# Two stores of the gradient of wo, split by partitions into two and three parts

## The chip, the core and the metric

The kernel is written in Bass with the Tile layer and runs on one core of one Trainium2 chip. Its time is the device time of one execution in microseconds; of the kernel before there are three such times, and one further execution was taken with the hardware profiler. A core has the engines PE (matmul), DVE, ACT and POOL, SP (which here only issues transfers), and 16 DMA engines, which move everything between the chip's memory (HBM) and the on-chip memory with its 128 partitions. SP and ACT each have a hardware queue for transfers (q1 and q10 in the profile), POOL has a software queue (q0); all three are served by the same 16 DMA engines.

## The reference

One transformer block for one decoded token, in bfloat16, forward and backward:

```
h  = x + attention(layernorm(x), k_cache, v_cache, wq, wo)      # 32 heads of 128, 4096 cached positions, batch 2
h2 = h + relu(layernorm(h) @ w1) @ w2                           # 640 -> 1728 -> 640
outputs: h2, and the gradients (for grad_out) of x, k_cache, v_cache, wq, wo, w1, w2
```

The caches are 67 MB each, and so are their gradients; the weights and their gradients are a few MB each. The gradient of wo is a matrix of 4096 x 640: for each batch the outer product of the attention output `o` (4096 long) with the gradient that reaches `h` (640 long), summed over the two batches.

## The kernel before, in words

Phase 1 runs over the 64 pairs of batch and head: it loads K and V of a pair (1 MB each), makes the scores, the softmax and the sums that the output needs. Phase 2 runs over the 64 pairs again in another order (`turns`): it takes V (`Wt`, loaded again except for twelve pairs that were kept), makes the gradient of the probabilities, and writes the gradients of V and K of the pair, `gV` and `gK`, 1 MB each, with `outer_half` on DVE (L843). These 128 stores are issued by POOL (L911 and L862) on the software queue, one after the other; a buffer of `gV` or `gK` is used again when its store has landed on all DMA engines.

Beside phase 2 run generators that a step counter advances by fixed rates (`bg_step`): `fin_gen` makes the gradients of the weights. It widens a column vector into rows (`rows_of`) and calls `outer_rows`, which fills an output tile `ot` by small matmuls (L972) and copies on ACT (L978), and stores it with a transfer that ACT issues (L981). `ot` has 128 partitions; for the gradient of wo (`out_5`) each partition holds 16 consecutive rows of one half of the matrix, and they go out in three groups that begin at c0 = 0, 6 and 12: 6, 6 and 4 rows of 640 numbers, that is 7680, 7680 and 5120 bytes per partition in one piece. The loop over `s0` does this for the two halves (L1009 to L1011). The order of all instructions is fixed when the program is built.

Loads are issued by SP (L463, L379, L1025), and so are the four short stores of the two small outputs (`store_row`, L664), each of 5 rows of 256 bytes. Every transfer of SP and ACT takes one of eight semaphores in turn, and waits until the transfer eight before it has landed. Each DMA engine that takes part in a transfer writes a small packet of 4 bytes to the semaphore when its share is done.

The lines that the text speaks of: L220 and L221 (two loads of 10 rows of 256 bytes at the start), L463 (`Kt`, `Vt`, `Wt`), L664, L843, L862, L911, L978, L981, L1009 to L1011.

Of the kernel before, what the change touches and what calls it, by code (L numbers as in the profile page):

```python
# [15 lines left out]
def kernel(  # L16
# [20 lines left out]
    nc = tc.nc  # L37

    B, Sq, D = A_x.shape
# [34 lines left out]
    def pst(shape, dtype, role, name):  # L74

        k = banks[role].pop(0)
        banks[role].append(k)
        return ps.tile(shape, dtype, tag=f"bank{k}", bufs=1, name=name)
# [11 lines left out]
    def take(tag, shape, name):  # L90
        assert free[tag] > 0, (tag, name)
        free[tag] -= 1
        k = homes[tag].pop(0)
        t = pools[k].tile(shape, BF16, tag=f"big{k}", bufs=1, name=name)
        home_of[id(t)] = (tag, k, t)
        return t
# [9 lines left out]
    def give(t, to=None, first=False):  # L106
        tag, k, _ = home_of.pop(id(t))
        to = to or goes_to(tag)
        owned[tag] -= 1
        owned[to] += 1  # L110
        free[to] += 1
        homes[to].insert(0 if first else len(homes[to]), k)
        given_at[k] = step[0]
# [8 lines left out]
    def rested(tag, n):  # L122

        return free[tag] > 0 and (forced[0] or step[0] >= given_at.get(homes[tag][0], -n) + n)
# [24 lines left out]
    def wait(n):  # L149

        end = step[0] + n * spread[0]
        while step[0] < end and not forced[0]:
            yield 0.0
        yield
# [763 lines left out]
    def rows_of(pool, col, n, name, tag):  # L918

        r = pool.tile([128, n * 128], BF16, tag=tag, bufs=2 if tag == "rD" else 1, name=name)  # L920

        def widen(c0):
            cn = min(4, n - c0)
            w = FIN["wide"][(c0 // 4) % 2]
            nc.scalar.copy(out=w[:, 0:cn, :, 0:B], in_=col[:, c0:c0 + cn, None, :].to_broadcast([128, cn, 4, B]))

        widen(0)
        yield
        yield
        for c0 in range(0, n, 4):  # L930
            cn = min(4, n - c0)
            w = FIN["wide"][(c0 // 4) % 2]
            o_busy.append(banks["o"][0])
            t = pst([128, 512], FP32, "o", "rw_ps")
            for k in range(cn):
                nc.tensor.matmul(t[:, k * 128:(k + 1) * 128], lhsT=w[:, k, :, :].rearrange("p q x -> p (q x)"),  # L936
                                 rhs=ident_bf[:], start=True, stop=True)
            nc.scalar.copy(out=r[:, c0 * 128:(c0 + cn) * 128], in_=t[:, 0:cn * 128])
            o_busy.pop(0)
            if c0 + 4 < n:  # L940
                widen(c0 + 4)
                yield 1.0
            yield 0.7
        FIN[name] = r

    FIN = {}
# [2 lines left out]
    spreading = [False]  # L949
    o_busy = []  # L950

    def outer_rows(L, r0, nrow, R, N, out_ap, cc):


        P = nrow // cc
        grp = max(1, min(cc, 4096 // N))
        out_v = out_ap.rearrange("(p c) n -> p c n", c=cc)
        for c0 in range(0, cc, grp):
            gn = min(grp, cc - c0)
            while not rested("f", 13):  # L960
                yield 0.0
            ot = take("f", [128, grp, N], "ot")
            todo = [(k, n0, min(512, N - n0)) for k in range(gn) for n0 in range(0, N, 512)]
            made = []
            for x in range(len(todo) + 1):
                if x < len(todo):
                    k, n0, nn = todo[x]
                    q = 32 * (fw[0] % 4)
                    o_busy.append(banks["o"][0])
                    o_ps = pst([128, 512], FP32, "o", "o_ps")  # L970
                    fw[0] += 1
                    nc.tensor.matmul(o_ps[0:P, 0:nn], lhsT=L[q:q + B, bass.ds(r0 + c0 + k, P, step=cc)],  # L972
                                     rhs=R[q:q + B, n0:n0 + nn], start=True, stop=True)
                    made.append((o_ps, k, n0, nn))
                    yield 0.3
                if x > 0:
                    o_ps, k, n0, nn = made[x - 1]
                    nc.scalar.copy(out=ot[0:P, k, n0:n0 + nn], in_=o_ps[0:P, 0:nn])  # L978
                    o_busy.pop(0)
                    yield 0.3  # L980
            nc.scalar.dma_start(out=out_v[:, c0:c0 + gn, :], in_=ot[0:P, 0:gn, :])  # L981
            give(ot)

    def fin_gen(fin):
        FIN["wide"] = [fin.tile([128, 4, 4, 32], BF16, tag="wide", bufs=2, name="wide") for _ in range(2)]
        for w in FIN["wide"]:
            nc.vector.memset(w[:], 0.0)
        yield from wait(2)
        yield from rows_of(fin, acol, NF, "ar", "rX")
        ar_ps = pst([128, NFF, B], FP32, "mid", "ar_ps")  # L990
        for cf in range(NFF):
            nc.tensor.matmul(ar_ps[:, cf, :], lhsT=FIN["ar"][0:B, bass.ds(cf, 128, step=NFF)], rhs=ident_bf[0:B, 0:B],
                             start=True, stop=True)
        nc.scalar.copy(out=arow[:, 0:NFF, :], in_=ar_ps[:])
        if F_rem:
            nc.scalar.copy(out=arow[:, NFF, :], in_=acol[:, NFF, :])
        yield ("arow", 0)
        yield from rows_of(fin, gc, ND, "gr", "rD")
        yield from outer_rows(FIN["ar"], 0, NFF * 128, FIN["gr"], D, out_7[0:NFF * 128, :], NFF)
        if F_rem:  # L1000
            yield from outer_rows(FIN["ar"], NFF * 128, F_rem, FIN["gr"], D, out_7[NFF * 128:Dff, :], 1)
        yield from rows_of(fin, ghfc, NF, "ghfr", "rX")
        yield from rows_of(fin, x2c, ND, "x2r", "rD")
        yield from outer_rows(FIN["x2r"], 0, D, FIN["ghfr"], Dff, out_6, ND)
        HH = H // 2
        while ("gh1", B - 1) not in done:
            yield
        yield from rows_of(fin, gh1c, ND, "gh1r", "rD")
        for s0 in range(0, H, HH):  # L1009
            yield from rows_of(fin, OFc[:, s0:s0 + HH, :], HH, "OFr", "rX")  # L1010
            yield from outer_rows(FIN["OFr"], 0, HH * 128, FIN["gh1r"], D, out_5[s0 * 128:(s0 + HH) * 128, :], HH)  # L1011
        yield from rows_of(fin, x1c, ND, "x1r", "rD")
        for s0 in range(0, H, HH):
            while not all(("go", B - 1, h) in done for h in range(s0, s0 + HH)):
                yield
            yield from rows_of(fin, GQc[:, s0:s0 + HH, :], HH, "GQr", "rX")
            yield from outer_rows(FIN["x1r"], 0, D, FIN["GQr"], HH * 128, out_4[:, s0 * 128:(s0 + HH) * 128], ND)
# [165 lines left out]
    for n, (i, j) in enumerate(plan):  # L1183
# [29 lines left out]
        if i is None and ("w1", 1) in done and fin is None:  # L1213
            wts.release()
            fin = tc.alloc_tile_pool(name="fin", bufs=1)
            big2 = tc.alloc_tile_pool(name="big2", bufs=1)
            more_home("f", big2)
            banks.update(sps=[2, 3], o=[4, 5, 6])
            bg2.append(("fin", fin_gen(fin)))
            bg3.append(("gx", gx_gen(fin)))  # L1220
# [23 lines left out]
        at = LIGHT if j is None else HEAVY_TAIL if open_tail else HEAVY  # L1244
# [63 lines left out]
```

## Time and profile before

| | |
|---|---|
| three runs | 891.62, 892.14 (median), 892.43 us |
| the profiled execution | 892.4 us, of which the span from the first to the last instruction is 890.6 us |
| busy in the span | PE 83%, DVE 77%, ACT 53%, POOL 23% |
| DMA | 361.84 MB in 56304 packets, 404 GB/s over the span |
| stores of `ot` | 19, issued by ACT from 568.2 to 843.2 us |

The profile has the busy time of every engine in 40 slices of the span, the share of the DMA engines that was busy and what they moved, the chain of waits that ended last, groups of instructions, and the transfers with their time from issue to landing. Times in the text are from the start of the span. The DMA share is a mean over the 16 DMA engines, so one engine alone shows as 0.06. Beneath the profile's views the trace has a record of every DMA packet: start, duration, queue and bytes. It does not name the DMA engine.

### The profile page before, as it was taken

Reading aid. Unit: us, or ns where it says so; the run is one execution under the profiler, and the core shown is the slowest. Engines: PE = TensorE matmul, PEld = TensorE weight load, DVE = VectorE, ACT = ScalarE, POOL = GpSimd, SP = SyncE. Lnnn points to the kernel's source line nnn. Section 1 sums busy time; section 2 is a strip of 40 time slices with the busy share of each in tenths; the row PEclk is TensorE's granted clock in tenths of the full one; section 3 lists DMA queues with packets and bytes.
Section 4 is the critical chain, followed back from the end, with each engine's and each line's share of the span. In section 5 each row is a group of like instructions: output and inputs, shape, how many; then the busy total and the mean of one; then the engine's idle time right before and its main releaser. Section 6 shows DMA issues by size and latency. Waiting matters only on the chain. (4 is left out here: it accounts for less than half of the span.)

```text
span 890.6 us, 24645 instructions
## 1 busy us (share of the span) xinstructions
PE 740.5 (83%) x10145; PEld 622.4 (70%) x10145; DVE 687.8 (77%) x1283; ACT 469.7 (53%) x1184; POOL 204.3 (23%) x342
## 2 busy tenths in 40 slices
PE   4999899999999998888888767885888888658871
PEld 4887788888887887777777656764666665536561
DVE  2665779876789897796796888786988467899992
ACT  1344334443455665454547766554567766437751
POOL 1344434342310000000023321121323011111141
PEclk9999989999999999997995555555557765555555
DMA  9999999999889999999999999999999999999995
GB/s 377 419 411 404 409 407 419 410 415 408 350 325 369 422 422 424 422 421 424 422 390 423 420 419 420 419 416 416 391 404 413 424 425 425 424 426 424 423 421 245
DMA packets 56304, 361.84 MB, mean 406 GB/s; under 512 B 5696, under 2 KB 11904, under 8 KB 15488
## 3 DMA queue, kind: packets, MB, share of 16 engines
q1 hardware_dynamic: 34536, 211.13, 58.1%
q0 software_dynamic: 18432, 134.23, 36.2%
q10 hardware_dynamic: 3224, 14.92, 4.1%
q8 instruction: 80, 1.31, 0.6%
q14 instruction: 32, 0.26, 0.1%
HBM read 211.11 MB, written 149.13 MB: 404 GB/s over the span
## 5 line engine op out<-in xcount | busy, mean ns | idle before, releaser
L447 ACT COPY t_sb<-t_ps 128x512 f32<-128x512 f32 x479 | 273.1, 587 | 186.3 <-PE t_ps L442 181.7
L455 PEld LDWEIGHTS <-t_sb 128*128 128x128 bf16 x4096 | 169.9, 103 | 83.7 <-ACT t_sb L447 42.3
L442 PE MATMUL t_ps<-ident_f,Wt 128*128 128x128 f32 x832 | 201.0, 393 | 0.4 <-ACT t_sb L447 0.4
L483 DVE TENSOR_TENSOR pk<-Kt,ep 128x2048 bf16<-128x2048 bf16 x128 | 156.2, 1221 | 44.7 <-ACT ep L534 24.9
L476 PE MATMUL m_ps<-pk,Vt 128*128 128x129 bf16 x2048 | 176.1, 223 | 13.3 <-DMA Vt<-in_A_v_cache_dram 12.6
L843 DVE TENSOR_TENSOR gK<-rb,gsp 128x2048 bf16<-128x2048 bf16 x128 | 153.8, 1226 | 28.0 <-DMA out_dram<-gV 26.2
L843 DVE TENSOR_TENSOR gV<-rb,pp 128x2048 bf16<-128x2048 bf16 (+2 forms) x128 | 147.1, 1172 | 30.8 <-DMA out_dram<-gK 24.0
L442 PEld LDWEIGHTS t_ps<-ident_f,Wt 128*128 128x128 f32 x832 | 140.4, 205 | 31.9 <-issue 25.0
L442 PE MATMUL t_ps<-ident_f,Kt 128*128 128x128 f32 x1024 | 154.7, 287 | 4.6 <-DMA Kt<-in_A_k_cache_dram 4.5
L476 PEld LDWEIGHTS <-Vt 128*128 128x128 bf16 x2048 | 131.0, 99 | 16.9 <-DMA Vt<-in_A_v_cache_dram 14.9
L442 PEld LDWEIGHTS t_ps<-ident_f,Kt 128*128 128x128 f32 x1024 | 117.0, 148 | 6.1 <-issue 3.4
L493 POOL COPY pk<-ep 128x16 bf16<-128x16 bf16 x80 | 83.1, 1041 | 151.3 <-ACT ep L534 112.7
L455 PE MATMUL dp_ps<-gom,t_sb 128*128 128x2 bf16 x2048 | 96.0, 168 | 23.3 <-ACT t_sb L447 22.9
L911 POOL DMA_DIRECT2D out_dram<-gV x64 | 34.3, 536 | 307.8 <-DVE nb L526 114.3
L455 PE MATMUL s_ps<-gom,t_sb 128*128 128x2 bf16 x2048 | 80.2, 164 | 1.2 <-DVE t_sb L445 1.2
L862 POOL DMA_DIRECT2D out_dram<-gK x64 | 34.1, 533 | 202.0 <-DVE gK L843 156.8
L593 ACT CAST MT<-m_ps 128x128 bf16<-128x128 f32 x64 | 17.1, 266 | 116.3 <-PE m_ps L476 116.3
L978 ACT CAST ot<-o_ps 128x512 bf16<-128x512 f32 (+3 forms) x152 | 67.0, 498 | 9.7 <-DMA out_dram<-ot 8.5
L883 ACT ACTIVATE rb<-dp_ps,rt 128x256 bf16<-128x256 f32 x64 | 30.2, 472 | 46.5 <-PE dp_ps L878 44.8
L669 DVE CUSTOM_DVE_ANT_0 rows<-wo_t,rows 128x640 bf16<-128x640 bf16 x64 | 52.3, 817 | 0.4 <-ACT rows L647 0.2
L669 DVE CUSTOM_DVE_ANT_0 rows<-wqs,gqr 128x1024 bf16<-128x1024 bf16 x40 | 48.8, 1219 | 0.2
L669 DVE CUSTOM_DVE_ANT_0 rows<-w_t,rows 128x640 bf16<-128x640 bf16 (+2 forms) x58 | 45.8, 790 | 1.2 <-ACT rows L647 0.5
(194 smaller groups left out, 720.4 us busy)
## 6 DMA issues: line engine op xcount, KB each, us to landing
Kt<-in_A_k_cache_dram SPq DMA_DIRECT2D x64, 1024.0 KB, 16.4
Vt<-in_A_v_cache_dram SPq DMA_DIRECT2D x64, 1024.0 KB, 16.6
out_dram<-gV POOLq DMA_DIRECT2D x64, 1024.0 KB, 15.1
out_dram<-gK POOLq DMA_DIRECT2D x64, 1024.0 KB, 15.4
Wt<-in_A_v_cache_dram SPq DMA_DIRECT2D x52, 1024.0 KB, 11.8
out_dram<-ot ACTq DMA_DIRECT2D x6, 960.0 KB, 12.4
wq_t<-in_A_wq_dram SPq DMA_DIRECT2D x5, 1024.0 KB, 11.0
wqs<-in_A_wq_dram SPq DMA_DIRECT2D x5, 1024.0 KB, 16.1
```

The lines of the kernel that those rows point to most:

```text
L442: nc.tensor.transpose(t_ps[:, j, :], natf[:, 2 * cc:2 * cc + 2, :].rearrange("p c k -> p (c k)"), ident_f[:])
L447: nc.scalar.copy(out=t_sb[:], in_=t_ps[:])
L455: nc.tensor.matmul(dst[:, sc:sc + 2], lhsT=v[:, j, :, par], rhs=vecs[:, par, :], start=(par == 0), stop=(par == 1))
L476: nc.tensor.matmul(r["m"][:, 0:129], lhsT=r["V"][:, sc, :], rhs=r["pk"][sc // HALF][:, sc % HALF, 0:129], start=(sc == 0), stop=(sc == NSC ...
L483: nc.vector.tensor_tensor(out=p["pk"][k][:, :, 0:128].rearrange("p s (a two) -> p s a two", two=2), in0=p["K"][:, sl, :].rearrange("p s (a ...
L493: nc.gpsimd.tensor_copy(out=col, in_=e)
L669: nc.vector.tensor_tensor_reduce(out=junk[0:kc, 0:width], in0=in0, in1=in1, scale=1.0, scalar=0.0, op0=ALU.mult, op1=ALU.add, accum_out=acc)
L843: nc.vector.tensor_tensor(out=pairs_view(dst[:, sl, :]), in0=row.rearrange("p (a two) -> p a two", two=2)[:, None, :, :].to_broadcast([128 ...
L862: nc.gpsimd.dma_start(out=natural(out_2, bp, hp), in_=gK[:])
L883: nc.scalar.activation(out=rb[:], in_=bank[:, 128:384], func=ACT.Copy, scale=rt[:, b, h:h + 1])
L911: nc.gpsimd.dma_start(out=natural(out_3, b, h), in_=gV[:])
L978: nc.scalar.copy(out=ot[0:P, k, n0:n0 + nn], in_=o_ps[0:P, 0:nn])
```

## The change

In the first half of the gradient of wo (`s0 == 0`) the store of the second group (c0 = 6) goes out as two transfers, of partitions 0 to 118 and 119 to 127, and that of the third group (c0 = 12) as three, of partitions 0 to 48, 49 to 112 and 113 to 127. The same bytes go to the same places. All parts are issued by ACT, one right after the other, where the one store was. All other instructions stand on each engine in the order in which they stood; ACT has three transfers more. The eight semaphores of the hardware queues are handed on from there by one and then by three places further.

```diff
+    CUTS = {6: (0, 119, 128), 12: (0, 49, 113, 128)}
+
-    def outer_rows(L, r0, nrow, R, N, out_ap, cc):
+    def outer_rows(L, r0, nrow, R, N, out_ap, cc, cuts=()):
...
-            nc.scalar.dma_start(out=out_v[:, c0:c0 + gn, :], in_=ot[0:P, 0:gn, :])
+            at = dict(cuts).get(c0, (0, P))
+            for p0, p1 in zip(at, at[1:]):
+                nc.scalar.dma_start(out=out_v[p0:p1, c0:c0 + gn, :], in_=ot[p0:p1, 0:gn, :])
             give(ot)
...
-            yield from outer_rows(FIN["OFr"], 0, HH * 128, FIN["gh1r"], D, out_5[s0 * 128:(s0 + HH) * 128, :], HH)
+            yield from outer_rows(FIN["OFr"], 0, HH * 128, FIN["gh1r"], D, out_5[s0 * 128:(s0 + HH) * 128, :], HH,
+                                  CUTS if s0 == 0 else ())
```

## The prediction

> **What bounds the kernel now.** I read the 40 slices first. The DMA row stands at 9 from the first slice to the last but one; in the last it falls to 5, although stores are still owed. So I cut the end into stretches.
>
> ```profile
> 690.00:720.00 30.00, 24.95 (x277) 19.87 (x274) 12.39 (x13) 21.18 (x40) 3.40 (x8) 0.67 1.01 425
> ...
> 874.00:880.00 6.00, 0.00 (x0) 0.00 (x0) 0.61 (x1) 0.00 (x0) 0.53 (x1) 0.50 1.02 423
> 880.00:882.60 2.60, 0.00 (x0) 0.00 (x0) 0.00 (x0) 0.00 (x0) 0.00 (x0) 0.50 0.43 180
> 882.60:888.50 5.90, 0.00 (x0) 0.00 (x0) 0.00 (x0) 0.00 (x0) 0.00 (x0) 0.50 0.06 26
> ```
>
> The last two columns are the DMA share and GB/s. Nothing computes after 875 us, and from 882.60 to 888.50 the share is 0.06, one engine of sixteen, at 26 GB/s. One DMA engine ends 5.9 us after the other fifteen, and the kernel waits for it.
>
> Is that an accident of the end? I took the semaphore landings of each `gV` and `gK` store. In all 47 that land after 690 us the last of the 16 engines is 2.2 to 9.6 us behind the last but one, and the lead never closes, so it is one engine throughout. Its queue never runs dry: the next store is always issued at least 11.0 us before this engine ends the present one. The chain of waits ran through these landings already:
>
> ```profile
> 752.75 32.53 DMA out_dram<-gV
> 785.38 1.23 DVE gK L843
> ...
> 803.34 31.36 DMA out_dram<-gV
> ```
>
> Hence from 690 us on each microsecond more or less on that one engine moves the end by as much.
>
> Which engine is it? The packet records name none, but on a busy engine each packet starts 3 or 4 ns before its predecessor ends, so an engine's sequence can be followed back from the last packet. The late one runs back to 797 us without a gap over 20 ns, with eight data packets and one semaphore packet for each `gV` or `gK` store, and on the way it does this (us, ns, queue, bytes):
>
> ```
> 867.27  334  q0  8192
> 867.60   18  q1   256
> 867.62  319  q0  8192
> 867.93    9  q1     4
> ```
>
> The 256-byte packet is one row of a five-row store (L664). The late engine carries a row of each of the four such stores (801.58, 802.58, 867.60, 871.21 us), and the same four other engines carry the rest.
>
> How many engines a transfer uses is in the packet counts (the second line: queue, packets, MB, share):
>
> ```profile
> DMA packets 56304, 361.84 MB, mean 406 GB/s; under 512 B 5696, under 2 KB 11904, under 8 KB 15488
> ...
> q10 hardware_dynamic: 3224, 14.92, 4.1%
> ```
>
> Under 512 B are the 40 rows of 256 bytes of the six short transfers and the semaphore packets, 5656. POOL's 128, SP's 208 and ACT's 21 transfers at 16 each would make 5712; with 10 for each ten-row load (L220, L221) and 5 for each five-row store it is 351 x 16 + 2 x 10 + 4 x 5 = 5656 exactly. So a transfer gives equal shares: 128 rows to 16 engines by 8, 64 to 16 by 4, 10 to 10, 5 to 5, and always the same five.
>
> **The change, part by part.** Equal shares leave 119 rows (7 x 17) only 7 engines, 49 rows 7, 9 rows 9, 15 rows 15, 64 rows 16. A fixed choice that grows with the row count is one counted from an end of a list; then the five lie within every larger set, and the late engine within the seven. In rows of 7680 and of 5120 bytes, where each engine had 8 and 8: the seven get 17 + 1 = 18 and 7 + 4 + 1 = 12; the next two 1 and 5; six get 0 and 5; one 0 and 4.
>
> A packet of 7680 bytes takes 291 ns (716 of the 768 in the `ot` stores), less the 3 ns overlap 288; one of 5120 bytes 196, so 193; a semaphore packet 9, so 6. The page's rate agrees: 425 GB/s over 16 is 26.6 bytes per ns, 289 and 193 ns. For the late engine: 10 x 288 + 4 x 193 + 3 x 6 = 3670 ns, **3.7 us more**. The others of the seven end by 882.60 + 3.67 = 886.3, still before it. The relief elsewhere (7 x 288 + 3 x 193 = 2.6 us to 8 x 288 + 4 x 193 = 3.1 us) goes to engines that nobody waits for: worth nothing.
>
> Both stores lie where the lag already stands, and the lag lasts to the end:
>
> ```profile
> 698.21 0.34 ACTq L981 DMA_DIRECT2D out_dram<-ot  x1
> ...
> 719.82 0.34 ACTq L981 DMA_DIRECT2D out_dram<-ot  x1
> ```
>
> Three more issues on ACT cost 3 x 0.34 = 1.0 us of its queue. Behind them stand copies of `t_sb` (L447), then PE's `dp_ps`, DVE's `gsp` and the `gK` store; ACT is busy 21.18 of 30 us here, and the POOL queue is 11 us deep on the late engine, so nothing. Each part also waits for the hardware transfer eight before it. The 9-row part waits for a load issued at 675.70, long landed; the 49-row part for one issued at 691.83, landed by 704.8. The 64-row part waits for the 119-row part: the old store's rows ran from 701.89 to 708.93, 0.88 us a row beside the other queues, so 18 rows end near 717.7, before 719.82. The 15-row part waits for a load that landed at 716.3 and may slip by 8 x 0.29 = 2.3 us to 718.6. Both are covered by 1 to 2 us; without that cover ACT would stop for about 2 us, which the 11 us still hide. SP's later transfers wait for other semaphores than before, again eight back; none of those lands later than its waiter by these numbers. The buffers of the two tiles are next filled after 739 us: free.
>
> [...]
>
> Sum: 892.4 + 3.7 = 896.1 us for the profiled execution. It lies 0.03% above the median of 892.14, so 895.8 us for the median. If the late engine is as slow on these rows as on its `gV` and `gK` packets (320 ns on average after 797 us, others 309 to 313), the step is 3.8; with 0.5 us either way from shifted order the likeliest case alone gives 895.3 to 896.5.
>
> **Rivals.** (1) Faster: the late engine is outside the seven. Then it ends 2.6 to 3.1 us earlier, at 885.4 to 885.9, and the seven by 886.3, so the kernel gains 2.2 to 2.6 us: 889.8 us. It decides if the choice of 7 does not contain the choice of 5. Against it stand the four five-row stores on one set of engines; for it, that no transfer here shows 7.
>
> [...]
>
> (2) No difference: uneven shares over all 16, at most 8 + 1 and 4 + 4 + 1 rows per engine, so 0.29 + 0.19 = 0.5 us: 892.6 us. Against it: no transfer in the counts is uneven.
>
> (3) Much slower: with 17 rows in a run an engine reads partitions that other engines are reading too, and they slow each other. Single packets show the size: the longest of 7680 bytes took 664 ns instead of 291. If all 30 rows of the late engine doubled, 18 x 288 + 12 x 193 = 7.5 us would come on top (903 us); with half of that, 899.5 us. Against it: the 64-row store (L981, rows of 1280 bytes, four to an engine) ran at 55 ns a row like the 128-row one.
>
> **How the numbers follow.** A measurement here can tell about 0.2% (1.8 us) from no change. Forecast 0.70, rival 3 0.08, rival 2 with other ways to lose the step in slack 0.09, rival 1 0.13. Slower is 0.70 + 0.08 = 0.78, no difference 0.09, faster 0.13. The range reaches down to no change and up to rival 3 at nearly half, 892.0 to 899.0; outside lie rival 1 and the dearer part of rival 3, 0.17.
>
> **What would show it.** Right: the stretch with a share of 0.06 ends about 3.7 us later, ACT has 22 stores of `ot`, and packets under 512 B grow by 7 + 9 + 7 + 16 + 15 - 32 = 22 to 5718, q10 to 3246. Sixteen engines for every part would give 5744. Wrong: a last engine that ends earlier, or a tail in which several engines end together.

## The result and the profile after

| | before | after |
|---|---|---|
| median of 6 runs each | 892.28 us (890.84 to 894.08) | 900.97 us (899.52 to 904.30) |
| ratio, 95% interval | | 1.0104 [1.0081, 1.0128] |
| the profiled execution, its span | 892.4, 890.6 us | 901.18, 899.4 us |

The changed kernel is slower by 8.7 us by the medians (9.3 us by the ratio). The forecast was slower by 3.7 us (895.8, range to 899.0). Below, a ratio is turned into us by the time of the kernel before in the same session (892.3 to 893.4 us).

First the steps of the prediction that the page can answer: the packet counts and ACT's stores (page and timeline of the changed kernel; the issues have moved from L981 to L985).

```profile
DMA packets 56326, 361.84 MB, mean 402 GB/s; under 512 B 5718, under 2 KB 11926, under 8 KB 15510
...
q10 hardware_dynamic: 3246, 14.92, 4.1%
```

```profile
698.63 1.92 ACTq L985 DMA_DIRECT2D out_dram<-ot  x2
...
722.60 2.96 ACTq L985 DMA_DIRECT2D out_dram<-ot  x3
```

5718 and 3246 are the counts forecast for 7, 9, 7, 16 and 15 engines. Then the stretches (us from the start: length, busy time by engine, clock, DMA share, GB/s).

```profile
690.00:720.00 30.00, 26.42 (x227) 20.72 (x227) 12.13 (x18) 19.49 (x37) 2.62 (x6) 0.50 1.01 387
720.00:750.00 30.00, 22.76 (x224) 16.98 (x223) 17.51 (x20) 16.91 (x40) 4.69 (x10) 0.61 1.01 412
...
882.60:888.50 5.90, 0.00 (x0) 0.00 (x0) 1.31 (x2) 0.00 (x0) 0.53 (x1) 0.50 1.01 419
888.00:891.40 3.40, 0.00 (x0) 0.00 (x0) 0.00 (x0) 0.00 (x0) 0.00 (x0) 0.50 0.55 229
891.40:897.20 5.80, 0.00 (x0) 0.00 (x0) 0.00 (x0) 0.00 (x0) 0.00 (x0) 0.50 0.06 27
```

Two things. The stretch with one engine alone (share 0.06) is there again and about as long: the last `gK` store lands on its last engine at 897.69 us and on the last but one at 891.43 us; before it was 888.92 and 882.95 us. So not one engine is later but all sixteen: the last but one by 8.5 us, where the prediction had 3.7. (How much of this stood there before the first cut store is told under `before_again`.) And in the two stretches where the cut stores run the DMA share is the same 1.01 as before while the rate has fallen from 425 to 387 and 412 GB/s: the engines are as busy, and move less. By these rates that is 38 x 30 + 13 x 30 = 1530 KB, or 3.6 us at 425 GB/s. The second stretch in the kernel before:

```profile
720.00:750.00 30.00, 26.28 (x236) 18.36 (x237) 22.76 (x27) 19.32 (x47) 4.85 (x10) 0.56 1.01 425
```

The packets say how. In the two cut stores (queue q10) and in the `gV`/`gK` stores beside them (q0), from the trace's packet records:

```
store of 7680-byte rows   before: mean 291 ns, longest  313;  after: mean 388, 27 of 128 over 370, longest 1948
store of 5120-byte rows   before: mean 196 ns, longest  202;  after: mean 230,  9 of 128 over 300, longest  879
q0, 8192 bytes, in the first of the two   before: mean 311;   after: mean 371, 62 of 394 over 400
```

The chain of waits does not tell the two kernels apart. DMA has 23% of the span in the changed kernel and 18% in the kernel before, but 24% in a second profile of the kernel before (`before_again`). The changed kernel, then the second profile of before:

```profile
DMA 23%; DVE 10%; PE 8%; issue 5%; ACT 2%; POOL 0%; ACTq 0%; POOLq 0%; DVEq 0%
```

```profile
DMA 24%; DVE 9%; PE 7%; issue 4%; ACT 3%; POOL 0%; ACTq 0%; POOLq 0%; DVEq 0%
```

### The profile page after: what moved, and what is told of

The parts are those of the page before. It is cut to its first block, busy times and chain, and to the rows that moved or that the text cites. A ratio compares the mean times of both kernels' runs of the same rounds, so it can differ in the third digit from the quotient of the medians.

```text
span 899.4 us, 24648 instructions
## 1 busy us (share of the span) xinstructions
PE 744.0 (83%) x10145; PEld 623.7 (69%) x10145; DVE 687.4 (76%) x1283; ACT 469.8 (52%) x1184; POOL 202.6 (23%) x342
## 2 busy tenths in 40 slices
DMA packets 56326, 361.84 MB, mean 402 GB/s; under 512 B 5718, under 2 KB 11926, under 8 KB 15510
## 3 DMA queue, kind: packets, MB, share of 16 engines
q10 hardware_dynamic: 3246, 14.92, 4.1%
## 5 line engine op out<-in xcount | busy, mean ns | idle before, releaser
L442 PE MATMUL t_ps<-ident_f,Wt 128*128 128x128 f32 x832 | 203.5, 397 | 0.4 <-ACT t_sb L447 0.4
L442 PE MATMUL t_ps<-ident_f,Kt 128*128 128x128 f32 x1024 | 152.3, 284 | 5.3 <-DMA Kt<-in_A_k_cache_dram 4.8
L442 PEld LDWEIGHTS t_ps<-ident_f,Kt 128*128 128x128 f32 x1024 | 115.2, 147 | 6.9 <-issue 5.1
```

The costliest lines, as they stand in the source:

```text
L442: nc.tensor.transpose(t_ps[:, j, :], natf[:, 2 * cc:2 * cc + 2, :].rearrange("p c k -> p (c k)"), ident_f[:])
```

## The experiments

Three theories were set against each other: **A**, the late engine pays for its extra rows alone (288 and 193 ns each), as forecast; **B**, rows of the split stores collide with rows that other engines move (their packets take much longer than usual), on top of A; **C**, the parts cost by their number (issues, shifted semaphores). All results, with "late rows" for the price of the late engine's extra rows by A, and "slow" for the packets over 370 ns of the 7680-byte store and over 300 ns of the 5120-byte store (128 packets each; `twice` has 256):

| kernel | rows of the two stores | late rows, us | slow | ratio [95%] | us |
|---|---|---|---|---|---|
| changed, again | 119, 9 / 49, 64, 15 | 3.7 | 36 / 8 | 1.0095 [1.0070, 1.0121] | +8.5 |
| only_119 | 119, 9 / 128 | 2.9 | 27 / 0 | 1.0063 [1.0045, 1.0080] | +5.6 |
| only_49 | 128 / 49, 64, 15 | 0.8 | 0 / 0 | 1.0008 [0.9997, 1.0020] | +0.7 |
| only_49, again | the same | 0.8 | 0 / 3 | 1.0018 [1.0006, 1.0030] | +1.6 |
| equal16 | 16, 112 / 32, 16, 80 | 0 | 31 / 17 | 1.0023 [1.0008, 1.0037] | +2.0 |
| twice | 128, 128 / 128, 128 | 3.9 | 0 / 0 | 1.0056 [1.0041, 1.0071] | +5.0 |
| half64 | 64, 64 / 128 | 0 | 35 / 0 | 1.0011 [1.0000, 1.0022] | +1.0 |
| evenodd | even, odd / 128 | 0 | 0 / 0 | 0.9996 [0.9984, 1.0009] | -0.4 |
| colcut | 128 in six pieces / 128 | 0.2 | 0 / 0 | 1.0006 [0.9997, 1.0016] | +0.5 |
| half64_second | 128 / 64, 64 | 0 | 0 / 34 | 0.9995 [0.9981, 1.0009] | -0.4 |
| half64_then_49 | 64, 64 / 49, 64, 15 | 0.8 | 22 / 22 | 1.0021 [1.0006, 1.0036] | +1.9 |
| cut49_first | 49, 64, 15 / 128 | 1.2 | 29 / 0 | 1.0023 [1.0009, 1.0037] | +2.0 |
| cut119_second | 128 / 119, 9 | 1.9 | 0 / 11 | 1.0047 [1.0028, 1.0065] | +4.2 |
| first1 | 17, 15, 96 / 128 | 4.6 or -0.3 | 27 / 0 | 1.0015 [0.9998, 1.0033] | +1.3 |
| first3 | 51, 13, 64 / 128 | 4.0 or -0.9 | 25 / 0 | 1.0033 [1.0018, 1.0048] | +2.9 |
| first4 | 68, 12, 48 / 128 | 3.7 or -1.2 | 30 / 1 | 1.0047 [1.0028, 1.0066] | +4.2 |
| first5 | 85, 11, 32 / 128 | 3.5 or -1.7 | 31 / 0 | 1.0078 [1.0056, 1.0099] | +7.0 |

### Each cut alone, equal shares, and the bytes alone

```diff
+    CUTS = {6: (0, 119, 128)}                          # only_119
+    CUTS = {12: (0, 49, 113, 128)}                     # only_49
+    CUTS = {6: (0, 16, 128), 12: (0, 32, 48, 128)}     # equal16
+            if again and c0 > 0:                       # twice: both stores whole, two times over
+                nc.scalar.dma_start(out=out_v[:, c0:c0 + gn, :], in_=ot[0:P, 0:gn, :])
```

> Only the store of the second group (c0 = 6) is split, 119 and 9 rows; the third stays whole. Theory A (the late DMA engine pays for its extra rows alone, each at 288 ns): 18 rows for 8, so 2.9 us over the kernel before. Theory B (the extra rows, and on top the rows of the split store collide with the rows that other engines move, as the packets of 400 to 1950 ns between 702 and 722 us of the changed kernel suggest): 2.9 us plus nearly all of the 5 us that the whole change had over theory A, so 6 to 8 us. Theory C (the number of transfers or the shifted semaphores cost, not the shares): one of the three added transfers, so about a third of 8.7, 2.9 us.

> Only the store of the third group (c0 = 12) is split, 49, 64 and 15 rows; the second stays whole. Theory A: 4 rows of 5120 bytes more on the late engine, 0.8 us. Theory B: 0.8 us plus a tenth of the collisions, 1 to 2 us. Theory C: two of the three added transfers, about 5.8 us.

> As many parts as in the changed kernel, at the same places, but of 16 and 112, and of 32, 16 and 80 rows, so that every engine still has 8 rows of each store. Theory A: no extra rows, 0 us. Theory B: 0 us if equal shares keep each engine on rows that no other engine needs at that time; up to 5 us if leaving the order of the 128-row transfer is enough for collisions, and then packets of over 400 ns show in the two stores. Theory C: the same three transfers and the same shift of semaphores, so 8.7 us.

> Nothing is split; the second and the third store of the first half are each sent a second time, whole, to the same place with the same bytes. Every engine, the late one too, gets 8 more rows of 7680 and 8 of 5120 bytes in the order of the 128-row transfer: 8 x 288 + 8 x 193 = 3.9 us of work, a little more than the 3.7 us of the change. Theories A and B: 3.9 us, with no packet over 400 ns. Theory C: two added transfers, about 5.8 us. If an engine's added work is not worth as much at the end, it is less than 3.9.

`twice` gives each engine 8 more rows of both stores, with no cut and with no packet of either store over 314 ns: +5.0 us [3.7, 6.3] for the 3.9 of A. It is not a clean measure of the bytes, though. ACT issues each second copy only when the first has landed, 11.6 and 11.1 us later, and stands still meanwhile; the loads fall differently, and after 695 us 104 load packets of 8192 bytes (q1) take over 400 ns, where the kernel before has 1. In one stretch the rate falls to 252 GB/s (421 in the kernel before):

```profile
749.00:755.00 6.00, 5.44 (x46) 3.76 (x47) 5.18 (x6) 3.69 (x9) 0.53 (x1) 0.71 0.88 252
```

`only_49` adds two of the change's three extra transfers and gives +0.7 us where A has 0.8. So both runs agree with the term for bytes on a DMA engine, neither measures it alone, and C has nothing to pay for. `equal16` makes as many transfers as the change with no engine given a row more, and still costs 2.0 us, with slow packets in both stores: that is B without A. `only_119` is B on top of A: 5.6 us for 2.9.

### The same cuts once more, and which engines

```diff
+    CUTS = {6: (0, 119, 128), 12: (0, 49, 113, 128)}   # after_again, as changed
+    CUTS = {6: (0, 17, 32, 128)}                       # first1: 1, 15, 16 engines
+    CUTS = {6: (0, 51, 64, 128)}                       # first3: 3, 13, 16
+    CUTS = {6: (0, 68, 80, 128)}                       # first4: 4, 12, 16
+    CUTS = {6: (0, 85, 96, 128)}                       # first5: 5, 11, 16
```

> The changed kernel once more, beside the next three. Theory A (the late engine pays for its 10 and 4 extra rows alone): +3.7 us. Theory B (as A, and rows of the split stores and of transfers beside them collide, as only_119 and equal16 showed): +8 to +9 us, as in its first result. The sum of only_119 (+5.6) and only_49 (+0.7) lies between, at +6.3: if this run comes out near +6.3, the two cuts simply add; near +9, the second cut costs more behind the first.

> The store of 7680-byte rows alone is cut, into 17, 15 and 96 rows: by equal shares the first engine of the list gets 17 + 1 + 6 = 24 rows instead of 8, the next fourteen 7, the last 6. If the late engine is the first of the list: 16 x 288 ns = +4.6 us by A, more by B. If it is not: by A a gain of one row, -0.3 us, since the first engine, 4.6 us later than now, still ends before the late one; by B +1 to +2 us, the price of collisions without share, as in equal16 (+2.0 us).

> The store of 7680-byte rows alone is cut, into 51, 13 and 64 rows: the first three engines of the list get 17 + 1 + 4 = 22 rows instead of 8, the next ten 5, the last three 4. If the late engine is among the first three: 14 x 288 ns = +4.0 us by A, more by B. If it is the fourth or fifth: by A a gain of 3 rows, -0.9 us; by B that gain and collisions of 1 to 2 us, so 0 to +1. Together with first1 this places the late engine: first (both slower), second or third (only this one slower by over 4 us), fourth or fifth (neither).

> The store of 7680-byte rows alone is cut into 68, 12 and 48 rows: the first four engines of the list get 17 + 1 + 3 = 21 rows instead of 8, the next eight 4, the last four 3. After first1 (+1.2 us) and first3 (+2.7 us) the late engine is most likely the fourth or fifth. If the fourth: 13 x 288 ns = +3.7 us and 1 to 2 us of collisions, so +4.7 to +5.7 us. If the fifth: a gain of 4 rows, 1.2 us, and the collisions, so 0 to +1 us, or up to +2.7 as in first3 if the four engines with more rows become the last.

> The store of 7680-byte rows alone is cut into 85, 11 and 32 rows: the first five engines of the list get 17 + 1 + 2 = 20 rows instead of 8, the next six 3, the last five 2. If the late engine is among the first five, as the prediction has it from the five-row stores: 12 x 288 ns = +3.5 us for its rows, and 1 to 2 us of collisions, so +4.5 to +5.5 us. If it is not: a gain of 5 or 6 rows, 1.4 to 1.7 us, and the same collisions, so about no difference, unless the five engines with 3.5 us more and their collisions become the last.

The changed kernel repeats: +8.5 us. `first1` gives 16 more rows to the first engine and costs 1.3 us [-0.2, 2.9], not 4.6: the late engine isn't the first. `first5` costs 7.0 us [5.0, 8.8], over the 4.5 to 5.5 expected with the late engine among the five. If it were not among them, collisions would have had to cost the five at least 7.5 us (7.0 and their lead of 4.0 or 6.0 us, less 3.5 for their rows), more than in any run here. So it is most likely among the five, as the prediction read from the five-row stores. `first3` and `first4` fall between their two cases. In their profiles the last engine ends only 2.1 and 0.1 us behind the last but one (6.0 before): the engines that got more rows end together with the late one. Which of the second to fifth it is stays open.

### What makes rows collide

```diff
+    CUTS = {6: (0, 64, 128)}                           # half64
+                for p0 in range(2):                    # evenodd, at c0 == 6
+                    nc.scalar.dma_start(out=out_v[p0:P:2, c0:c0 + gn, :], in_=ot[p0:P:2, 0:gn, :])
+            step = 1 if cuts and c0 == 6 else gn       # colcut
+            for k0 in range(0, gn, step):
+                nc.scalar.dma_start(out=out_v[0:P, c0 + k0:c0 + k0 + step, :], in_=ot[0:P, k0:k0 + step, :])
```

> The store of 7680-byte rows alone is cut, into two halves of 64 rows: each of the sixteen engines gets 4 + 4 rows, as many as in one store of 128. A: no difference. B, if rows collide because an engine no longer reads the rows that it reads in a store of 128: packets of 7680 bytes well over 291 ns and +1 to +2 us, as in equal16. B, if rows collide only where a part has another number of rows than a power of two: packets of 291 ns and no difference.

> The store of 7680-byte rows alone is sent in two parts of 64 rows, as in half64, but the even rows first and the odd rows then. If the rows of a part go to the engines in order and in runs of four, engine e reads four of the same eight rows in each part that it reads in a store of 128, while in half64 it reads rows that belong to other engines there. Theory B1 (rows collide when an engine reads rows that another engine reads in the other stores): no packets far over 291 ns, no difference. Theory B2 (rows collide because a store goes in parts of fewer than 128 rows, whichever they are): slow packets as in half64 (35 of 128 over 370 ns) and about +1 us.

> The store of 7680-byte rows alone is cut by columns into three parts of 128 rows of 2560 bytes, so no row changes its engine; 3 issues instead of 1 and 256 more packets. B1 and B2: no collisions, packets near a third of 291 ns, about 100 ns, and no difference beyond 8 x 2 x 6 ns = 0.1 us. Theory C (parts cost for their number, by shifted semaphores and issues): slower by 1 us or more.

(`colcut` makes six pieces of 1280 bytes a row, not three of 2560 as its expectation has it.) The DMA part of the profile, 695 to 725 us in 40 slices of 0.75 us: busy tenths and GB/s. The changed kernel, `half64` and `evenodd`:

```profile
DMA  9999999999999999999998999999989999999999
GB/s 381 412 435 429 412 404 470 382 448 403 389 369 356 345 399 380 401 378 423 390 399 346 432 346 411 356 313 325 258 302 346 358 336 347 402 399 420 440 397 407
```

```profile
DMA  9999999999999999999999999899999999999998
GB/s 425 416 434 408 423 403 413 421 453 408 414 436 415 404 412 451 339 352 266 322 376 408 386 397 385 337 390 336 393 458 382 459 415 437 404 437 426 404 470 371
```

```profile
DMA  9999999999999999999999999999999999999999
GB/s 455 402 451 412 447 404 437 404 415 448 406 448 406 444 406 449 396 458 399 459 393 426 426 437 404 437 426 415 437 426 437 423 431 415 432 421 412 419 415 405
```

In all three the engines are busy throughout (8 or 9 tenths in every slice). In `half64` the rate drops to 266 to 408 GB/s from the 17th slice (707 us) to the 29th (717 us); its packets of 7680 bytes run from 705.7 to 716.8 us. In the changed kernel the dips last from 702 to 721 us, as long as the 119-row part, and reach 258. In `evenodd` no slice falls below 393. From 700 to 720 us, the changed kernel, `half64` and `evenodd`:

```profile
700.00:720.00 20.00, 17.80 (x158) 14.63 (x157) 6.98 (x7) 13.41 (x23) 1.47 (x4) 0.50 1.01 369
```

```profile
700.00:720.00 20.00, 17.75 (x163) 14.45 (x162) 8.07 (x9) 13.51 (x22) 2.61 (x6) 0.59 1.01 393
```

```profile
700.00:720.00 20.00, 15.64 (x207) 13.24 (x205) 8.01 (x9) 14.79 (x27) 2.62 (x6) 0.76 1.01 425
```

For `half64` and `evenodd` the time alone tells little: +1.0 us [0.0, 2.0] and -0.4 us [-1.4, 0.8]. The packets tell more. Both kernels send two parts of 64 rows, to 16 engines each by the counts (5712 packets under 512 B, 16 more than the 5696 before), so by equal shares with four rows for each engine in each. They differ only in which rows a part has: in `half64` 35 of 128 packets are slow, mean 429 ns; in `evenodd` none, mean 291 ns. And the six pieces of `colcut`, all 128 rows each, kept ACT's queue for longer than any cut and cost nothing that shows (packets at 55 ns, as in the kernel before's own 1280-byte rows):

```profile
698.48 8.53 ACTq L986 DMA_DIRECT2D out_dram<-ot  x6
```

So neither the number of parts nor their row count makes these collisions, but which rows a part has. That an engine is given rows that others are moving would be a reason, and is not shown: no record says which rows an engine gets. The runs leave another reading. The parts that ran clean (`evenodd`, `colcut`) reach over all 128 partitions, those that collide cover a block of neighbouring ones. The place in the on-chip memory was not tried apart from the place in HBM either, since the two go together in all these kernels.

Slow packets are not peculiar to cut stores. In the profile of the kernel before, where no store is cut, 201 packets of `gV` and `gK` stores and 113 load packets of 8192 bytes took over 400 ns between 400 and 695 us; from 695 us on it has 12 and 1. So the experiments show what a cut adds in a stretch that is otherwise nearly free of them, not why packets are slow in general.

### Which store, which cut, which order

```diff
+    CUTS = {6: (0, 49, 113, 128)}                      # cut49_first
+    CUTS = {12: (0, 64, 128)}                          # half64_second
+    CUTS = {6: (0, 64, 128), 12: (0, 49, 113, 128)}    # half64_then_49
+    CUTS = {12: (0, 119, 128)}                         # cut119_second
```

> The cut into 49, 64 and 15 rows, on the store of 7680-byte rows, and the other store whole. The late engine gets 7 + 4 + 1 = 12 rows instead of 8: 4 x 288 ns = +1.2 us. Theory D1 (the store decides whether a cut collides): slow packets of 7680 bytes as in the other cuts of this store, and +1 to +2 us on top, so +2.2 to +3.2 us. Theory D2 (the cut decides, and 49, 64, 15 doesn't collide): packets of 291 ns and +1.2 us.

> The cut into two halves of 64 rows, on the store of 5120-byte rows, and the other store whole. D1: packets of 196 ns, as in only_49, and no difference. D2: slow packets as in half64 and about 2/3 of its cost, +0.7 us.

> The first store in halves of 64 rows, the second in 49, 64 and 15. If the costs of half64 (+1.0 us) and only_49 (+0.7 us) simply add: +1.7 us, and packets of 196 ns in the second store. Theory D3 (the second cut collides only behind a store that has set the engines apart): 8 or more packets of 5120 bytes over 300 ns, as in the changed kernel, and +2.5 to +4 us.

> The cut into 119 and 9 rows, on the store of 5120-byte rows, and the other store whole. The late engine gets 18 rows instead of 8: 10 x 193 ns = +1.9 us. D1: packets of 196 ns and +1.9 us. D2: slow packets as in only_119, whose price above its share was 2.7 us, here about 2/3 of it: +3.7 us in all.

> The same kernel as only_49. After cut49_first (slow packets, +2.0 us) and half64_second (34 slow packets of 5120 bytes, no difference in time) neither the store nor the cut decides whether rows collide. If chance does, by how the engines stand in that execution: slow packets of 5120 bytes this time are likely, and a time between +0.7 and +2 us. If this cut on this store never collides alone: none over 300 ns again, and +0.7 us.

> The kernel before once more, for its profile: packets of 7680 and 5120 bytes in the two stores at 291 and 196 ns with none over 370 and 300, as in its first profile, if the collisions come from the cuts alone. The last landing of a gV or gK store before the first cut store (the 81st, at 685.8 us in the first profile and 684.8 to 689.7 us in the other kernels) shows how much of a difference between two profiles is there before the cuts.

Neither the store (D1) nor the cut (D2) decides: the cut into 49, 64 and 15 rows collides on the first store (29 slow packets), and 64 and 64 rows collide on the second (34). Whether the second cut needs another one ahead of it (D3) stays open. Behind a cut it showed 9, 8 and 22 slow packets (the changed kernel twice, `half64_then_49`), alone 3 in its second profile and none in its first; but the time of `half64_then_49`, +1.9 us [0.5, 3.2], is nearer to the sum (1.7) than to D3's 2.5 to 4. How many packets are slow changes from execution to execution of one kernel (0 and 3). The kernel before, profiled again, had none in the two stores.

`half64_second` is the one to note: 34 slow packets, and no difference in time. `cut119_second` has 11 and costs 2.3 us more than its bytes. Collisions between engines that were ahead would eat only their lead. That is argued: the last engine ends 3.6 us behind the last but one here, and 6.0 and 4.0 us in the two profiles of the kernel before, which is too close to show it.

One caution came with `before_again`. At the 81st landing of a `gV` or `gK` store, ahead of any cut, the two profiles of the kernel before stand at 685.8 and 684.9 us, the two of the changed kernel both at 689.5, and the other kernels between 684.8 and 689.7. So 3.7 us of the 8.8 us between the shown profiles were there before the first cut store was issued. Counted from that landing to the last one, the two profiles of the changed kernel took 208.2 and 211.3 us, the two of the kernel before 203.1 and 203.0: 5.1 to 8.4 us more. The sizes here therefore come from the timed runs, and from the profiles mainly what kind of loss it is. No run was faster than the kernel before by more than its interval.

## Why the prediction was right and wrong

**Right.** That equal shares leave 119 rows to 7 engines and 49 rows to 7: the counts are those forecast, to the packet (5718 and 3246). That the late engine lies among the seven: in the changed kernel's profile it can be followed. Its semaphore packets of two stores in a row are known, eight rows of `gV` or `gK` lie between them, and each packet starts 3 or 4 ns before the one ahead of it ends. From 701.6 to 724.2 us that gives one sequence without a break, with 18 rows of 7680 bytes, as forecast. So rival 1 is out; `first5`, +7.0 us, speaks for the set of five. Rival 2 is out by the counts. That ACT's three more issues cost nothing: `colcut` issues five more, for 8.5 us of ACT's queue, and is at +0.5 us [-0.3, 1.4]. (The cover of 1 to 2 us that the prediction counted on did not hold: the three issues took 2.96 us, and 6.86 us in `after_again`, instead of 1.0. But every `gV` and `gK` store after 690 us was still issued 10.5 us or more before the late engine was through with the one ahead of it.)

**The size of the byte term** (3.7 us) agrees with the runs: the 18 rows are there, `twice` gave 5.0 for 3.9 (its interval from 3.7), and the two runs of `only_49` 0.7 and 1.6 for 0.8. No run measures it alone.

**The step that failed** is the one that left collisions at nothing. The sum took every row at its usual 288 or 193 ns; in the two cut stores the packets took 388 and 230 ns on average, against 291 and 196 before, and rows of other stores slowed beside them. The sum had no term for that, and rival 3, which has rows slow each other, got 0.08 on the strength of one row: the 64-row store of L981, at 55 ns a row like the 128-row one. That row did not bear so far. Its 1280-byte packets are short, and it says nothing of packets of 7680 and 5120 bytes beside full `gV` and `gK` stores; `half64` cuts such a store into the same 64 rows, and 35 of its packets are slow. The trace of before could not price it, for no store in it sends long rows in blocks of less than 128; a cost that cannot be seen should have been put into the sum with a lower and an upper bound, not into a rival.

**How much.** What each run cost beyond its late rows: 1.0, -0.4 and 2.0 us with equal shares (`half64`, `half64_second`, `equal16`), 2.7 and 2.3 us for 119 and 9 rows (`only_119`, `cut119_second`), 4.8 and 5.6 us for the change. The same sequence of the late engine's packets gives its own loss in the changed kernel's profile: up to 724.2 us eight of its packets took over 40 ns longer than usual, together 2.7 us, and up to 742.3 us (with one break in the sequence) 3.4 to 3.6 us; in the kernel before it is 0.3 us from 697 to 726 us. With the bytes that is 3.7 + 3.5 = 7.2 us. Its landing of the 89th store, at 742.3 us, is 52.8 us behind its 81st, where the two profiles of the kernel before have 45.9 and 45.4: 6.9 to 7.4 us more. So the term that was left out was about as large as the one that was in the sum. What came after 742 us is not accounted for like this.

A mean over the engines is a weaker estimate. The rows of 5120 bytes and more of the three queues that took over 40 ns longer than usual lost 90 us after 695 us in the changed kernel's profile, and 7 us in that of before. Over 16 engines the difference is 5.2 us, and 3.7 + 5.2 = 8.9 us against the measured 8.7. That this fits so well is luck. 16 us of the 90 lie in 47 load packets from 803 to 819 us, far behind the cut stores, and the same working is too dear for most of the other kernels: 1.7 us for `half64`, which cost 1.0, 1.8 us for `half64_second`, which cost nothing, 3.6 us for `equal16`, which cost 2.0.

**The rival's own price** was closer than the forecast: "with half of that, 899.5 us". Half of its 7.5 us is 3.75 us, near the 3.4 to 3.6 us that the late engine lost by slow packets. What its picture left out: the packets that slowed were not only those of the late engine's 30 rows, but rows of `gV` and `gK` stores on other engines too (62 of 394).

**Open:** whether the two cuts add. Alone they cost 5.6 us [4.0, 7.1] and 0.7 to 1.6 us, together 8.5 to 9.3 us; the intervals meet, so a price for the pair is not shown. Which of the second to fifth engine is the late one, and why it is late. And why rows collide at all: what is shown is that with the same number of rows in each part 35 packets were slow in `half64` and none in `evenodd`.

## What to carry to other kernels

Where a kernel ends with its DMA engines full, a store is more than its bytes: cut into blocks of neighbouring rows, it can slow its own packets (here from 291 to 388 ns on average) and those of other transfers (311 to 371 ns), and the share of busy time did not show it here (1.01 before and after), only the GB/s (425 and 387) and the packet durations did. If a store must go in parts, cut it by columns or into alternate rows; neither cost anything that shows here (`colcut` +0.5 us [-0.3, 1.4], `evenodd` -0.4 us [-1.4, 0.8], one kernel each). And when a change makes a pattern that the trace has never shown, its cost belongs into the sum with both bounds; a far-off row that looks harmless is no reason for zero.

## What the runs showed of the hardware

- A packet of 7680 bytes that takes 291 ns in the kernel before (716 of 768) took up to 2313 ns (`first5`) when its store was cut into blocks of rows; equal shares had slow packets as well as uneven ones (64 and 64 rows, `half64`: 35 of 128, up to 1751 ns). Whole transfers have slow packets too (201 of `gV` and `gK` over 400 ns between 400 and 695 us in the kernel before).
- Two 64-row stores of alternate rows ran like one of 128 (`evenodd`): mean 291 ns, no packet over 315 ns.
- 34 slow packets of 5120 bytes cost nothing that shows in time (`half64_second`: 0.9995 [0.9981, 1.0009]), and how many there are changed between executions of one kernel (`only_49`: 0 and 3; the changed kernel: 27 and 36 in its first cut store).
- The DMA share stood at 1.01 whether packets were slow or not: 425, 393 and 369 GB/s in `evenodd`, `half64` and the changed kernel from 700 to 720 us.
